# VectorE instead of adding DMAs for the low parts of chunk 1's second weight group and of chunk 6's GELU products

## The chip, the cores and the metric

The kernel runs on 1 core of one Trainium2 chip. The metric is the device time of one execution in microseconds (us), less is better. The kernel before took 605.02 us in the median of 3 runs (604.14 to 605.84).

The core has five engines that work side by side, each through its own list of instructions in order: TensorE (PE in the profile, its weight loads PEld), VectorE (DVE), ScalarE (ACT), GpSimd (POOL) and SyncE (SP). SP does nothing here but issue DMAs; POOL issues them too. An instruction waits for what it reads to be written and for the buffer that it writes to be free, and everything behind it on its engine waits with it.

## What is computed

The reference mixes two branches over the same input x (2048 tokens, 512 channels) with a gate for each token:

```python
x = A_x
g = _sigmoid((x * gate_w).sum(-1, keepdims=True))
a = _A_ref(x, A_wqkv, A_wo)                      # 32 heads of 16, 8 keys per query, 2 apart
b = _B_ref(x, B_w_gate, B_w_up, B_w_down)        # (gelu(x @ w_gate) * (x @ w_up)) @ w_down
return g * a + (1 - g) * b
```

`_A_ref` is an attention in which each query looks at 8 keys (itself and 7 earlier ones, every second token). `_B_ref` is a feed-forward layer with 1792 hidden channels. All is float32.

## The kernel before

**Two parities.** The tokens are split into even and odd ones (`par` 0 and 1), 1024 each, since the attention never crosses them. For each parity the kernel makes keys, queries and values, and then runs the feed-forward layer (`ffn(par)`), while VectorE works on attention in the background (scores L519 and L522, softmax L533 to L544, mixing L558 to L571). In the profile `ffn(0)` lies between about 50 and 283 us.

**High and low parts.** TensorE multiplies in a float32 format of reduced precision. So each operand is split into a high part (the number rounded to that format) and a low part (the rest), and a product is three matmuls: high by high, high by low, low by high. Where weights are split in `product`, the third matmul of each three is the first to use the weight's low part.

The low part is made in one of two ways:
- By VectorE: ACT copies the number to the high part, then VectorE subtracts that from the number.
- By an adding DMA: ACT copies the negated number to the place of the low part, POOL issues a DMA that adds the number to it, and ACT makes the high part with a second copy.

**Chunks.** `ffn` goes over 14 chunks (`f` = 0 to 13) of 128 hidden channels. A chunk is computed with a Strassen scheme in 7 products instead of 8; the weights of a chunk are therefore combined first (`combine`, three subtracts at L657 on VectorE) into seven pieces in two groups: `t1, t2, b11` (group 0) and `b21, t3, b22, t4` (group 1, 128x1024 elements). `operands(par, f, i)` splits group `i` of chunk `f` into tile `g0` or `g1`, in two steps. It is called one chunk ahead: the first step of group 1 is placed after the product `t1` and a piece of other work, the second after `s4`. In parity 0 group 0 is split by VectorE (L677, L681) and group 1 by an adding DMA (L685, L688, L690). Parity 1 reads group 0 back from DRAM, where parity 0 had stored it (`keep_parts`, L703), and its combined group 1 too (`keep`, L697).

**Buffers and queues around it.** The raw weights of a chunk lie in a tile `raw`, of which there are two. `fetch(f + 2)` (L647) loads the next but one into the same buffer, so it waits until chunk `f`'s last reader is done, the adding DMA and the store of `keep` included. SP issues that load, the loads `r` of the down weights (`fetch_d`, L651), the stores and the attention's loads in one queue. The adding DMAs are issued by POOL, whose transfers show as queue q0; SP's show as q1. POOL also issues adding writes of keys and queries to DRAM in chunks 0 and 1 (`key_one`, L465 and L466).

**GELU.** `gate_up` does the seven products of a chunk. L826 and L842 apply GELU to the gate's half, `add` (L740, L741) makes the up half. `hidden(par, (f, b), ge, up)` multiplies the two (L745) for each half `b` of the tokens and splits the product into `hh` and `hl`: for chunks in `LOWS[par]` by an adding DMA (L751 to L753), for others by VectorE (L748, L749). `down` (L776) multiplies them by the down weights `d`, a pair of chunks at a time; those are split in `down_w` by an adding DMA (L719, L720, L722), in the first chunks by VectorE (L715, L717).

**What sets the order.** The program text names no engine order by hand here: a scheduler orders the instructions on each engine. `paced` only keeps an instruction from being moved ahead of the last matmul emitted before it. A change of one instruction can therefore change the order of all that follow.

Of the kernel before, what the change touches and what calls it, by code (L numbers as in the profile page):

```python
# [33 lines left out]
LOAD = 4.0  # L34
BT = 4
MASKED = -1e9 * DH ** 0.5
LOWS = (4, 6, 8, 10), (4, 6, 8, 10, 12)


GROUPS = (("t1", "t2", "b11"), ("b21", "t3", "b22", "t4"))  # L40
# [5 lines left out]
def tile_gated_mix(ctx: ExitStack, tc: tile.TileContext, xt, wqkv, wff, wo, out):  # L46
# [11 lines left out]
    def tl(tag, dt=F32):  # L58
        return pool.tile([P, COLS.get(tag, 512)], dt, name=tag, bufs=BUFS[tag])
# [521 lines left out]
    def paced(ins):  # L581

        if PIN[0] and ins.ins.engine == mybir.EngineType.DVE:
            tc.keep_in_program_order(ins)
        if not PACING[0]:
            return ins
        tc.add_manual_dep(ins.ins, LAST[-1].ins.name, mybir.DependencyInfo(mybir.DependencyClass.Sync,
                          mybir.DependencyReason.SCHED_ONLY), reason="pace")
        return ins
# [72 lines left out]
    def operands(par, f, i):  # L662


        n = len(GROUPS[i]) * QW
        w = tl(f"g{i}", F32R)
        hi, lo = w[:, :n], w[:, n:2 * n]
        for k, op in enumerate(GROUPS[i]):
            WG[f, op] = hi[:, k * QW:(k + 1) * QW], lo[:, k * QW:(k + 1) * QW]
        if par and not i:  # L670
            nc.sync.dma_start(w[:, :2 * n].bitcast(F32), WS[f, i])
            yield
            return
        raw = RAW[f][:, 3 * i * QW:][:, :n]
        if not i:
            KEEP[f] = w[:, :2 * n]
            ins = nc.scalar.activation(hi, raw, AF.Copy)  # L677
            if f:
                paced(ins)
            yield  # L680
            ins = nc.vector.tensor_tensor(lo, raw, hi.bitcast(F32), op=OP.subtract)  # L681
            if f:
                paced(ins)
            return
        ins = nc.scalar.activation(lo, raw, AF.Copy, scale=-1.0)  # L685
        if par and not f:
            paced(ins)
        nc.gpsimd.dma_start(lo.bitcast(F32), raw, accum_op=OP.add)  # L688
        yield
        ins = nc.scalar.activation(hi, raw, AF.Copy)  # L690
        if par or f:
            paced(ins)
# [51 lines left out]
    def hidden(par, key, ge, up):  # L744
        nc.vector.tensor_tensor(ge, ge, up, op=OP.mult)  # L745
        hh_, hl_ = tl("hh", F32R)[:, :512], tl("hl", F32R)[:, :512]
        if key[0] not in LOWS[par]:
            nc.scalar.activation(hh_, ge, AF.Copy)  # L748
# [138 lines left out]
    def ffn(par):  # L887
        todo = iter(())
        for f in range(FC):
# [9 lines left out]
            if f + 1 < FC:  # L899
                for i in range(2):  # L900
                    steps = operands(par, f + 1, i)
                    at(1 + 2 * i, next, steps, None)
                    at(5 + i, next, steps, None)
                at(0 if f != 1 else 5, fetch_d, f + 1)
                for g_ in ((), (0, 1))[f] if f < 2 else (f,):
                    steps = down_w(par, g_)
                    at(2 if f > 2 else 4 - f % 2, next, steps, None)
                    at(7, next, steps, None)
            else:
                steps = down_w(par, f)  # L910
                at(1, next, steps, None)
                at(4, next, steps, None)
# [149 lines left out]
    for kc in range(KC):  # L1062
        name, i = ("b11", "b21")[kc // 2], kc % 2
# [134 lines left out]
    def first():  # L1198
        for _ in range(2):
            yield  # L1200
        combine(0)
        keep(0)
        for i in range(2):
            yield
            for _ in operands(0, 0, i):
                yield
        combine(1)
        fetch_d(0)
        yield
        for n in "t1", "b22":  # L1210
            room_b(n)
            for kc in range(2):
                if n == "t1":
                    combine_b("t1", "b11", "b22", "t2", kc)
                split_b(n, kc)
                yield
# [8 lines left out]
    def second():  # L1225

        yield from operands(1, 0, 0)
        room_v(*SMALL, *LARGE)
        for n in "b11", "b21", "t1", "b22", "t2":
            fetch_v(n)  # L1230
            yield
# [55 lines left out]
```

## Time and profile before

| | us |
|---|---|
| median of 3 runs | 605.02 |
| the profiled execution | 603.44 |
| its span, first to last instruction | 601.7 |
| TensorE busy | 589.1 |
| VectorE busy | 532.4 |
| ACT busy | 430.1 |
| POOL busy | 125.8 |

A row of the timeline has the start and the length in us, the engine, the line of the kernel and the operation, what it writes and reads, the shape and the count of equal instructions in a row; in square brackets stand the idle time before it and what ended that. Matmuls overlap: each is listed with its whole length, and the pace is read from start to start. The mean granted clock of TensorE over the span is 0.997 of full speed. The DMA rows have the queue, the packets, the MB moved and the time of the packets as a share of 16 DMA engines; shares of several queues can add to more than 100%, since packets of two queues overlap in an engine.

### The profile page before, as it was taken

What the parts mean: (1) busy time and instruction counts of PE and PEld (TensorE: products, weight loads), DVE (VectorE), ACT (ScalarE), POOL (GpSimd) and SP (SyncE); (2) the same over time, 40 slices, a digit from 0 to 9 for tenths busy, and PEclk for the clock granted to TensorE, in tenths of its full rate; (3) what the DMA queues carried; (4) which work ended last, traced back from release to release, by engine and by line L of the source; (5) the groups of instructions that cost most, each with busy time, mean ns of one, the idle gap of its engine ahead of it and who ended that gap; (6) DMA issues with size and microseconds to landing.
All of it is one profiled execution on the core that took longest, in us unless ns stands there. A gap on an engine that the chain in (4) does not pass through costs nothing.

```text
span 601.7 us, 8290 instructions
## 1 busy us (share of the span) xinstructions
PE 589.1 (98%) x2743; PEld 490.1 (81%) x2743; DVE 532.4 (88%) x619; ACT 430.1 (71%) x761; POOL 125.8 (21%) x147
## 2 busy tenths in 40 slices
PE   9999997999999999999999999999999999999997
PEld 7889885888878887888789888888888888887885
DVE  6979987999799998998896999799979988999891
ACT  6778783678796769767876665767696778796632
POOL 0131761112121202102100472112121212131200
PEclk9999999999999999999999999999999999999999
DMA  8689999988897979898889999689788988988724
GB/s 305 211 242 302 262 306 223 295 260 222 263 250 204 272 185 293 242 321 266 262 265 342 252 276 256 205 187 261 206 246 216 259 209 212 270 196 222 103 53 174
DMA packets 89896, 144.33 MB, mean 240 GB/s; under 512 B 8703, under 2 KB 50047, under 8 KB 89854
## 3 DMA queue, kind: packets, MB, share of 16 engines
q1 hardware_dynamic: 67470, 106.91, 54.5%
q0 software_dynamic: 22096, 36.51, 34.0%
q8 instruction: 21, 0.34, 0.2%
q10 hardware_dynamic: 288, 0.39, 0.2%
q14 instruction: 21, 0.17, 0.1%
HBM read 69.83 MB, written 46.49 MB: 193 GB/s over the span
## 4 chain that ended last, share of the span: by engine, by line
PE 78%; DMA 9%; issue 5%; ACT 5%; SPq 1%; DVE 1%; POOL 0%; POOLq 0%; ACTq 0%
PE p L729 35%; PE p L776 11%; PE acc L776 10%; PE acc L460 9%; PE p L1001 5%; DMA g<-raw 3%; PE acc L348 2%; PE p L348 2%; PE p L460 2%; PE acc L1001 2%; DMA r<-wff 1%; DMA raw<-ws 1%; DMA hl<-c 1%; DMA raw<-xt 1%; DMA raw<-wff 1%
## 5 line engine op out<-in xcount | busy, mean ns | idle before, releaser
L729 PE MATMUL p<-S,g 128*128 128x512 f32 x672 | 166.6, 389 | 0.2 <-ACT p L811 0.2
L729 PEld LDWEIGHTS p<-S,g 128*128 128x128 f32 x672 | 125.9, 188 | 26.6 <-ACT p L811 0.6
L729 PE MATMUL p<-A,g 128*128 128x512 f32 x504 | 127.4, 392 | 2.6 <-DMA g<-raw 2.6
L729 PEld LDWEIGHTS p<-A,g 128*128 128x128 f32 x504 | 95.4, 190 | 23.3 <-DMA g<-raw 3.4
L558 DVE TENSOR_TENSOR prod<-v,lg 128x2048 f32<-128x2048 f32 x32 | 72.9, 2279 | 0.9
L519 DVE TENSOR_TENSOR prod<-kq 128x2048 f32<-128x2048 f32 x32 | 73.0, 2280 | 0.3
L522 DVE TENSOR_REDUCE lg<-prod 128x128 f32<-128x2048 f32 x32 | 73.0, 2283 | 0.1
L776 PE MATMUL p<-d,hh 128*128 128x512 f32 x224 | 68.4, 390 | 1.9 <-ACT c L826 1.9
L688 POOL DMA_DIRECT2D g<-raw x28 | 24.2, 865 | 201.9 <-ACT g L685 142.3
L776 PE MATMUL acc<-d,hh 128*128 128x512 f32 x224 | 59.1, 391 | 0.0
L740 ACT ACTIVATE c<-p 128x512 f32<-128x512 f32 x56 | 33.5, 599 | 35.6 <-PE p L729 34.4
L776 PEld LDWEIGHTS p<-d,hh 128*128 128x128 f32 x224 | 42.0, 188 | 11.0 <-ACT c L826 2.4
L776 PEld LDWEIGHTS acc<-d,hh 128*128 128x128 f32 x224 | 42.0, 188 | 8.9 <-ACT hh L748 0.2
L741 DVE TENSOR_TENSOR c<-c,s 128x512 f32<-128x512 f32 x56 | 38.0, 686 | 10.4 <-ACT c L740 10.1
L745 DVE TENSOR_TENSOR c<-c 128x512 f32<-128x512 f32 x56 | 38.3, 686 | 5.2 <-ACT c L842 5.1
L776 PE MATMUL p<-d,hl 128*128 128x512 f32 x112 | 42.7, 390 | 0.0
L562 DVE TENSOR_TENSOR prod<-prod 128x1024 f32<-128x1024 f32 x32 | 39.1, 1221 | 0.3
L734 ACT ACTIVATE s<-p 128x512 f32<-128x512 f32 x56 | 33.0, 591 | 7.8 <-PE p L729 7.3
L720 POOL DMA_DIRECT2D d<-r x23 | 19.7, 857 | 88.5 <-ACT d L719 78.8
L789 ACT ACTIVATE rt<-p 128x512 f32<-128x512 f32 x48 | 28.3, 597 | 11.3 <-PE p L776 11.2
L460 PE MATMUL acc<-d,S 128*128 128x512 f32 x144 | 35.4, 390 | 0.6 <-ACT hh L1163 0.6
L776 PE MATMUL acc<-d,hl 128*128 128x512 f32 x112 | 34.9, 392 | 0.7 <-DMA hl<-c 0.7
(220 smaller groups left out, 1060.3 us busy)
## 6 DMA issues: line engine op xcount, KB each, us to landing
g<-raw POOLq DMA_DIRECT2D x28, 512.0 KB, 7.0
ws<-g SPq DMA_DIRECT2D x14, 768.0 KB, 7.5
g<-ws SPq DMA_DIRECT2D x14, 768.0 KB, 6.9
r<-wff SPq DMA_DIRECT2D x28, 256.0 KB, 4.6
raw<-wff SPq DMA_DIRECT2D x14, 512.0 KB, 4.4
d<-r POOLq DMA_DIRECT2D x23, 256.0 KB, 6.6
ws<-raw SPq DMA_DIRECT2D x14, 384.0 KB, 6.3
raw<-ws SPq DMA_DIRECT2D x14, 384.0 KB, 5.3
```

Of the source, the lines that this page charges most:

```text
L460: LAST[:] = [nc.tensor.matmul(ps, x[:, ts], w, start=(start and kc == i == 0), stop=(kc == 1 and i == 2), skip_group_check=True)]
L519: paced(nc.vector.tensor_tensor(prod, spans(k, jj), q[:, jj:jj + 2, None, :].to_broadcast([P, 2, W, UC]), op=OP.mult))
L522: nc.vector.tensor_reduce(two_of(lg, jj), prod.rearrange("p j w (h d) -> p (j w) h d", d=DH), axis=AX.X, op=OP.add)
L558: paced(nc.vector.tensor_tensor(prod.rearrange("p j w (h d) -> p (j w) h d", d=DH), spans(v, jj).rearrange("p j w (h d) -> p j w h d", d=D ...
L562: nc.vector.tensor_tensor(prod[:, :, :4], prod[:, :, :4], prod[:, :, 4:], op=OP.add)
L729: LAST[:] = [nc.tensor.matmul(ps, w_, a_, start=(start and kc == 0 and n == 0), stop=(kc == 1 and n == 2), skip_group_check=True)]
L734: nc.scalar.activation(s, ps, AF.Copy)
L740: nc.scalar.activation(c, ps, AF.Copy)
L741: nc.vector.tensor_tensor(c, c, s, op=OP.add)
L745: nc.vector.tensor_tensor(ge, ge, up, op=OP.mult)
L776: LAST[:] = [nc.tensor.matmul(pp, a[:, ts], w, start=(i == 0 and n == 0 and gr == 0), stop=(i == 1 and n == 2), skip_group_check=True)]
L1001: LAST[:] = [nc.tensor.matmul(pa, a, b, start=(first and n == 0), stop=(last and n == 2), skip_group_check=True)]
```

## The change

Group 1 of chunk 1 in parity 0 takes the same way as group 0: ACT copies to the high part in the first step, and VectorE subtracts in the second; the negated copy, the adding DMA and the later copy go. And chunk 6 leaves parity 0's list `LOWS`, so that both of its GELU products are split by VectorE. Parity 1 and all other chunks are as they were.

```diff
@@ -34,7 +34,7 @@
-LOWS = (4, 6, 8, 10), (4, 6, 8, 10, 12)
+LOWS = (4, 8, 10), (4, 6, 8, 10, 12)
@@ -674,6 +674,7 @@
         raw = RAW[f][:, 3 * i * QW:][:, :n]
         if not i:
             KEEP[f] = w[:, :2 * n]
+        if not i or (not par and f == 1):
             ins = nc.scalar.activation(hi, raw, AF.Copy)
             if f:
                 paced(ins)
```

From L677 on, a line of the kernel before has a number one higher in the kernel after.

## The prediction

> **What bounds the kernel now.** I read the page's busy times first, then TensorE's waits, then TensorE's timeline at the longest of them, then the clock by stretches.
>
> ```profile
> PE 589.1 (98%) x2743; PEld 490.1 (81%) x2743; DVE 532.4 (88%) x619; ACT 430.1 (71%) x761; POOL 125.8 (21%) x147
> ```
> ```profile
> PE p L729 <- DMA g<-raw: 2.6, 2, 1.5
> PE p L776 <- ACT c L826: 1.9, 1, 1.9
> PE acc L776 <- DMA hl<-c: 0.7, 1, 0.7
> ```
>
> TensorE is busy for all but 12.6 us of the span of 601.7, and the change touches no matmul. So the only gain is in TensorE's gaps, and the only loss is in new ones. The rows give total, times and longest; these three lie where the change acts or just behind it. The timeline of the worst place (start, length, engine, line, count):
>
> ```profile
> 92.25 0.61 PE L729 MATMUL p<-A,g 128*128 128x512 f32 x2
> 94.38 0.50 PE L729 MATMUL p<-A,g 128*128 128x512 f32 x1 [1.51 <-DMA g<-raw]
> ...
> 97.94 2.88 PE L729 MATMUL p<-S,g 128*128 128x512 f32 x12
> 100.66 0.39 PE L776 MATMUL acc<-d,hh 128*128 128x512 f32 x1
> 102.98 0.73 PE L776 MATMUL p<-d,hh 128*128 128x512 f32 x2 [1.93 <-ACT c L826]
> ...
> 105.36 4.05 PE L729 MATMUL p<-A,g 128*128 128x512 f32 x12
> 109.24 2.88 PE L729 MATMUL p<-S,g 128*128 128x512 f32 x12
> ```
> ```profile
> 100.00:104.00 4.00, 2.07 (x9) 1.40 (x8) 0.48 (x2) 2.19 (x5) 0.86 (x1) 1.00 0.50 197
> 104.00:108.00 4.00, 4.00 (x12) 3.16 (x11) 4.00 (x6) 2.34 (x4) 0.00 (x0) 0.57 0.88 206
> ```
>
> At full pace 12 matmuls start in 100.66 - 97.94 = 2.72 us, 0.227 each. The first gap is 94.38 - 92.25 less two matmuls: 1.68. The second is 102.98 - 100.66 less one: 2.09. Then comes a loss that no wait shows: from 104 to 108 the granted clock (third column from the end) is 0.57. From 102.98 to 109.24 run 20 matmuls, in 6.26 us for 4.53: 1.73 more. This place costs 1.68 + 2.09 + 1.73 = 5.5 us.
>
> The page "TensorE: Matmul & The Clock Gate" of the Trainium skill, section "Part 1: The HAM clock gate", says the clock halves after an idle window of about 3.4 us. Here a gap of 1.93 us, soon after one of 1.51, was followed by 0.57, so the trace does not need so long a gap. By the page's figure alone a shorter gap would cost no clock, and the place 3.8 us.
>
> **Why TensorE waits there.** The two gaps have one cause. POOL's, SP's and ACT's timelines:
>
> ```profile
> 58.88 0.86 POOL L688 DMA_DIRECT2D g<-raw  x1 [10.00 <-PE p L729]
> 80.22 0.89 POOL L688 DMA_DIRECT2D g<-raw  x1 [1.31 <-ACT g L685]
> ```
> ```profile
> 83.38 0.32 SPq L703 DMA_DIRECT2D ws<-g  x1
> 94.39 0.33 SPq L647 DMA_DIRECT2D raw<-wff  x1
> 94.77 1.34 SPq L651 DMA_DIRECT2D r<-wff  x2
> ```
> ```profile
> 101.81 0.63 ACT L719 ACTIVATE d<-r 128x512 fp32r<-128x512 f32 x1 [9.01 <-DMA r<-wff]
> 102.34 0.58 ACT L826 ACTIVATE c<-p 128x512 f32<-128x512 f32 x1
> ```
>
> The L688 issues at 58.88 and 80.22 are chunks 1 and 2. Chunk 2's adding DMA lands at about 94.3, and the third matmul of its "a12" product, the first to use a low part, starts at 94.38. SP's queue stands from 83.4 to 94.39 before L647, which needs the raw buffer that this DMA reads. Both r loads stand behind it, ACT's L719 waits 9.01 us for one, and the GELU L826 behind L719 frees TensorE's bank: the second gap.
>
> **The change, part 1: chunk 1.** Removed are one 128x1024 copy on ACT (L685) and one 0.52 MB adding DMA (58.88). The copy to the high part moves forward into L685's place; VectorE gets one 128x1024 subtract.
>
> ```profile
> L562 DVE TENSOR_TENSOR prod<-prod 128x1024 f32<-128x1024 f32 x32 | 39.1, 1221 | 0.3
> L749 DVE TENSOR_TENSOR hl<-c,hh 128x512 fp32r<-128x512 f32 x38 | 26.0, 686 | 1.9 <-ACT hh L748 1.9
> L685 ACT ACTIVATE g<-raw 128x1024 fp32r<-128x1024 f32 x28 | 29.5, 1054 | 4.4 <-DVE raw L657 2.3 <-DMA raw<-wff 2.0
> L751 ACT ACTIVATE hl<-c 128x512 fp32r<-128x512 f32 x18 | 11.3, 628 | 1.1 <-DVE c L745 1.1
> L752 POOL DMA_DIRECT2D hl<-c x18 | 16.8, 934 | 58.6 <-ACT hl L751 42.3 <-ACT hh L753 15.8 <-issue 0.6
> ```
>
> VectorE +1.22, ACT -1.05. In the changed program's order the subtract stands behind the second score reduction (63.29 below), so it ends near 66.7. TensorE's first use of it is in the product at 76.61: about 10 us of cover.
>
> ```profile
> 63.29 2.28 DVE L522 TENSOR_REDUCE lg<-prod 128x128 f32<-128x2048 f32 x1
> 78.70 0.95 DVE L681 TENSOR_TENSOR g<-raw,g 128x768 fp32r<-128x768 f32 x1
> ```
> ```profile
> 76.61 1.52 PE L729 MATMUL p<-A,g 128*128 128x512 f32 x6
> ...
> 84.09 1.07 PE L729 MATMUL p<-A,g 128*128 128x512 f32 x4
> ```
>
> What is queued behind it goes 1.2 us later. The nearest need is chunk 2's first low parts (L681, ending 79.65), used at 84.09: over 4 us of cover. Without that cover, each us late would be one on TensorE.
>
> What it frees is transfer time. The DMA rows (packets, MB, share of 16 engines) from 62 to 67 and 67 to 94, and chunk 2's issue (KB, us to landing):
>
> ```profile
> q0 software_dynamic: 144, 0.52, 52.5%
> ```
> ```profile
> q0 software_dynamic: 3830, 2.31, 62.5%
> q1 hardware_dynamic: 3262, 5.33, 57.2%
> ```
> ```profile
> g<-raw POOLq DMA_DIRECT2D x1, 512.0 KB, 14.1
> ```
>
> The 0.52 MB on q0 from 62 to 67 are chunk 1's DMA: 52.5% of 5 us = 2.6 us of all 16 engines. From 67 to 94 both queues together hold 120%: there is always work waiting, ending in chunk 2's 14.1 us. If all the freed time is passed on, chunk 2 lands 2.6 us earlier; if POOL's issue times set the pace, none. I take 1.8, nearer the full end, because the engines never run dry in between. ACT's copy for chunk 2 still stands just behind chunk 1's GELU L826, so its issue stays at about 80.
>
> The program's order on TensorE changes too: from chunk 1's last "S" products to that third matmul are 38 matmuls, not 43, so it is wanted 1.1 us sooner, at 92.70 - 1.13 = 91.6 (92.70 being 92.25 and two matmuls). From 94.4 to 91.6 are 2.8 us; less 1.8 leaves a gap of 1.0. One r load now stands before L647 on SP, and L826 before L719 on ACT. So the second gap has lost its cause, and with a gap of 1.0 I expect full clock: 4.5 of 5.5 us saved. Ends: all 2.6 passed on, 0.2 left, 5.3 saved; nothing passed on, a gap of 2.8 with 1.73 of clock, 1.0 saved.
>
> **Part 2: chunk 6.** Twice a 128x512 copy on ACT (0.63) and an adding DMA issued by POOL go; VectorE gets two subtracts of 0.69.
>
> ```profile
> 179.06 0.61 PE L729 MATMUL p<-A,g 128*128 128x512 f32 x2
> 180.32 1.19 PE L776 MATMUL acc<-d,hl 128*128 128x512 f32 x4 [0.65 <-DMA hl<-c]
> 181.35 0.62 PE L729 MATMUL p<-A,g 128*128 128x512 f32 x2
> ```
> ```profile
> 174.53 1.20 POOL L752 DMA_DIRECT2D hl<-c  x1
> ```
>
> Six matmuls take 2.29 us instead of 1.36: 0.9 lost to waiting for chunk 6's adding DMA. A subtract of 0.69 behind at most one attention step of 2.28 is sooner than the 5.8 us from that issue to that matmul. I take all 0.9; ends 0 and 0.9.
>
> **Part 3: the order.** No instruction is moved by hand, but from about 75 to 283 us nearly every engine's order differs. Besides the places above, that stretch loses this on TensorE:
>
> ```profile
> 233.04 0.61 PE L729 MATMUL p<-A,g 128*128 128x512 f32 x2
> 234.75 1.19 PE L729 MATMUL p<-A,g 128*128 128x512 f32 x4 [1.09 <-DMA g<-raw]
> ```
> ```profile
> 224.10 1.06 ACT L685 ACTIVATE g<-raw 128x1024 fp32r<-128x1024 f32 x1 [2.26 <-DVE raw L657]
> ```
>
> That is 1.71 less two matmuls, 1.3 us: VectorE combined chunk 11's weights late, so ACT and the adding DMA were late. A new order may keep this, lose it, or make another. I take 1.2 us of new loss, about one such event; ends: 1.3 gained, 6 lost (one more place like the first).
>
> **The sum.** 4.5 + 0.9 - 1.2 = 4.2 us. The profiled execution took 603.44 (span 601.7 and 1.74 around it), so 599.2 for its like. The median of the runs is 605.02, which gives 600.8.
>
> **Rivals.** (1) The transfer is not earlier: the first gap grows to 2.8 with slow clock and only the cascade behind it shrinks. For: the accumulating key and query writes ahead of chunk 2 on q0 are issued as TensorE yields them. Against: 120% from 67 to 94. Saved 1.0 + 0.9 - 1.2 = 0.7: 604.3, no change that can be told.
>
> (2) VectorE becomes the late engine. It is 88% busy and gets 2.6 us more. Place: chunk 11, where it already delays ACT by 2.26. If the combine is 2.6 later there, the gap grows from 1.3 to 3.9 and takes 1.73 of clock; a lag that reaches one more chunk costs a full 5.5. 4.5 + 0.9 - 2.6 - 1.73 - 5.5 = -4.4: 609.4. It decides once the third L657 of a chunk ends more than about 2 us behind ACT's readiness to copy. Against: VectorE has 69 us idle, and the 2.6 lie far before 224.
>
> Beside it, "SBUF — State Buffer" of the Trainium skill, section "Who interferes with whom", says that a VectorE instruction with two SBUF inputs contends with a GpSimd instruction that reads SBUF. The row of L752 above names no wait on VectorE, and I give it no price.
>
> **How the numbers follow.** Forecast 0.58, its own range 597.8 (5.3 + 0.9 and 1.0 of the old order's loss gone) to 603; rival 1 0.18; rival 2 0.20, in any size above 606.8 to 609.4 or lighter ones that only cancel the gain; 0.04 left. What a measurement can tell from no change is about 0.3%, 1.8 us. Faster takes the forecast and a fifth of rival 1: 0.62. Same takes most of rival 1 and the light cases of rival 2: 0.17. Slower: 0.21. The range 597.8 to 606.5 leaves out the heavy cases of rival 2 and little below.
>
> **What would show it.** Right: chunk 2's g<-raw lands by about 92.5, TensorE's wait for L826 is gone, no stretch near 104 has a clock under 1, and no wait for hl<-c near 180. Part 1 is wrong if that landing stays at 94. Part 3 is wrong if g<-raw or ACT waits over 2 us in all appear on TensorE between 110 and 283; if they follow L657, rival 2 holds.

## The result, and the profile after

| | before | after |
|---|---|---|
| median | 605.02 us | 597.30 us |
| lowest to highest of 5 runs | 601.82 to 606.29 | 596.79 to 598.35 |
| the profiled execution | 603.44 | 596.87 |
| its span | 601.7 | 595.1 |

The ratio is 0.9886, 95% interval 0.9861 to 0.991: faster, by 7.7 us between the medians and 6.6 us between the profiled executions. The forecast was 600.8 in a range of 597.8 to 606.5, so the direction was right; the median came out 0.5 us below the range, and by the ratio the time is 598.1, just inside it. Beside the experiments below, the kernel before had medians of 603.60 to 604.14 over 14 to 29 runs, so about 6.5 us is the safer figure for the gain.

The page of the kernel after, busy times:

```profile
PE 586.6 (99%) x2743; PEld 488.8 (82%) x2743; DVE 533.3 (90%) x622; ACT 429.4 (72%) x758; POOL 123.4 (21%) x144
```

VectorE is busy 0.9 us longer, TensorE 2.5 us shorter with the same 2743 matmuls: 1.7 of these are the low clock from 104 to 108 us before; where the rest lies isn't shown. Two of TensorE's waits (total, times, longest):

```profile
PE p L730 <- DMA g<-raw: 0.7, 1, 0.7
PE p L460 <- ACT p L434: 0.6, 1, 0.6
```

The waits for L826 and hl<-c are gone, and one of the two for g<-raw. TensorE's timeline at the place that was worst:

```profile
89.39 1.52 PE L730 MATMUL p<-S,g 128*128 128x512 f32 x6
90.74 0.61 PE L730 MATMUL p<-A,g 128*128 128x512 f32 x2
92.05 1.19 PE L730 MATMUL p<-A,g 128*128 128x512 f32 x4 [0.69 <-DMA g<-raw]
93.08 1.08 PE L777 MATMUL acc<-d,hh 128*128 128x512 f32 x4
```

The third "a12" matmul is wanted at 90.74 + 0.45 = 91.19 and starts at 92.05: a gap of 0.86 where there were 1.68 and 2.09. The stretches that answer to the two shown of before (column 3: TensorE's busy time; third from the end: granted clock):

```profile
100.00:104.00 4.00, 4.00 (x20) 3.30 (x19) 4.00 (x6) 1.70 (x3) 0.00 (x0) 1.00 0.72 174
104.00:108.00 4.00, 4.00 (x19) 3.34 (x18) 3.96 (x8) 3.33 (x6) 0.12 (x1) 1.00 0.97 349
```

Both are full, at full clock. The place now costs 0.86 us in place of 5.5. Further on, 110 to 283 us, in the kernel before and then in the kernel after:

```profile
110.00:283.00 173.00, 171.10 (x753) 140.71 (x752) 160.43 (x186) 132.37 (x221) 27.94 (x34) 1.00 0.91 255
```
```profile
110.00:283.00 173.00, 172.36 (x760) 142.18 (x759) 161.57 (x190) 134.40 (x223) 27.62 (x35) 1.00 0.90 254
```

The 0.64 us that the second lacks are the wait for L434 at the switch to parity 1, which the first has only after 283. So nothing is lost to chunks there any more, where before lost 1.9 (0.65 in chunk 6, 1.09 in chunk 11, the rest small).

**What moved.** POOL's, SP's and VectorE's timelines after:

```profile
81.10 0.89 POOL L689 DMA_DIRECT2D g<-raw  x1 [1.99 <-DMA v<-vs]
```
```profile
72.24 0.32 SPq L503 DMA_DIRECT2D v<-vs  x1
72.61 1.39 SPq L504 DMA_DIRECT2D v<-vs  x1
...
84.43 0.33 SPq L651 DMA_DIRECT2D r<-wff  x1
92.05 0.33 SPq L647 DMA_DIRECT2D raw<-wff  x1
92.48 0.41 SPq L651 DMA_DIRECT2D r<-wff  x1
```
```profile
65.85 1.22 DVE L682 TENSOR_TENSOR g<-raw,g 128x1024 fp32r<-128x1024 f32 x1
...
78.61 0.95 DVE L682 TENSOR_TENSOR g<-raw,g 128x768 fp32r<-128x768 f32 x1
```

Chunk 1's subtract ends at 67.07, and chunk 2's first low parts are no later than before (78.61 against 78.70). Chunk 2's adding DMA is issued 0.9 us later than before, yet lands 2.3 us earlier. The DMA rows from 62 to 67 us after show how:

```profile
q1 hardware_dynamic: 1656, 1.92, 105.4%
q0 software_dynamic: 8, 0.00, 1.0%
...
vs<-hh SPq DMA_DIRECT2D x5, 128.0 KB, 4.6
```

Before, chunk 1's DMA took 52.5% of the engines in this stretch, and SP's queue q1 these (same columns):

```profile
q1 hardware_dynamic: 695, 0.96, 53.2%
...
vs<-hh SPq DMA_DIRECT2D x2, 128.0 KB, 8.6
```

Without that DMA q1 moves twice the bytes, and the attention's stores vs<-hh land in 4.6 us instead of 8.6. The loads that follow those stores on SP (L503, L504) are issued at 72.24; before:

```profile
79.08 0.32 SPq L503 DMA_DIRECT2D v<-vs  x1
79.44 0.46 SPq L504 DMA_DIRECT2D v<-vs  x1
```

So 960 KB of loads that before were issued beside chunk 2's DMA (80.22) now go 7 us earlier, 9 us ahead of it.

The Trainium skill, "DMA: Bandwidth & Descriptors", section "Queues, rings and completion order", says that each DMA engine takes turns between the queues it has work for, packet by packet. The near equal halves of 52.5% and 53.2% while both queues had work agree with it.

### The profile page after: what moved, and what is told of

Same layout as the page of the kernel before. It is cut to its first block, busy times and chain, and to the rows that moved or that the text cites. A ratio compares the mean times of both kernels' runs of the same rounds, so it can differ in the third digit from the quotient of the medians.

```text
span 595.1 us, 8276 instructions
## 1 busy us (share of the span) xinstructions
PE 586.6 (99%) x2743; PEld 488.8 (82%) x2743; DVE 533.3 (90%) x622; ACT 429.4 (72%) x758; POOL 123.4 (21%) x144
## 4 chain that ended last, share of the span: by engine, by line
PE 90%; DMA 6%; DVE 1%; ACT 1%; issue 1%; SPq 0%; ACTq 0%; DVEq 0%
PE p L730 42%; PE p L777 13%; PE acc L777 12%; PE acc L460 10%; PE p L1002 5%; PE acc L348 3%; PE p L348 3%; DMA g<-raw 2%; PE acc L1002 2%; DMA v<-vs 1%; DMA raw<-ws 1%; PE p L460 1%; DMA vs<-hh 1%; DMA raw<-xt 1%; DVE raw L245 1%
## 5 line engine op out<-in xcount | busy, mean ns | idle before, releaser
L730 PE MATMUL p<-A,g 128*128 128x512 f32 x504 | 125.1, 390 | 0.7 <-DMA g<-raw 0.7
L730 PEld LDWEIGHTS p<-A,g 128*128 128x128 f32 x504 | 94.3, 188 | 20.8 <-DMA g<-raw 1.1
L460 PE MATMUL acc<-d,S 128*128 128x512 f32 x144 | 35.2, 390 | 0.6 <-ACT hh L1164 0.6
```

The lines of the kernel that those rows point to most:

```text
L460: LAST[:] = [nc.tensor.matmul(ps, x[:, ts], w, start=(start and kc == i == 0), stop=(kc == 1 and i == 2), skip_group_check=True)]
L730: LAST[:] = [nc.tensor.matmul(ps, w_, a_, start=(start and kc == 0 and n == 0), stop=(kc == 1 and n == 2), skip_group_check=True)]
```

## The experiments

All ratios are to the kernel before on the same chip; 0.001 is 0.6 us. The profile of a run is one execution.

### Each half alone

c1 changes only the condition in `operands`; c6 changes only `LOWS`.

```diff
+        if not i or (not par and f == 1):      (c1)
+LOWS = (4, 8, 10), (4, 6, 8, 10, 12)           (c6)
```

> Chunk 1's half of the change alone; chunk 6 keeps its adding DMAs. If chunk 1 carries the gain (theory): at the place near 92 us TensorE waits about 0.7 us for g<-raw, no wait for L827, no clock under 1, and 4.6 us or more are gained: ratio to before 0.989 to 0.993. A wait for hl<-c in chunk 6 may be there, up to 0.9 us. Rival, that chunk 6's half or the two together make the gain: ratio 0.996 or more.

> Chunk 6's half alone. Theory: the place of chunk 2 is as before, a gap of about 1.5 us for g<-raw, one of about 1.9 for L826 and a clock near 0.57 behind it; only up to 0.9 us near 180 and what the new order behind it does are gained: ratio 0.996 to 1.000. Rival, that chunk 6's half carries a good part: ratio 0.994 or less.

c1: 596.61 us median (596.46 to 599.95), ratio 0.9905 (0.9876 to 0.9935). c6: 602.73, ratio 0.9998 (0.9979 to 1.0017). Chunk 1's half carries the whole gain, and chunk 6's gives nothing that can be told. One thing of c1 was not as expected: its profile, at 599.95 the slowest of its 6 runs, has a gap of 1.85 us for g<-raw instead of about 0.7, with a clock of 0.89 and 0.68 in the two stretches from 92 to 100 us. The wait for L827 is gone in it. c6's waits on TensorE:

```profile
PE p L776 <- ACT c L826: 1.9, 1, 1.9
PE p L729 <- DMA g<-raw: 1.7, 1, 1.7
PE p L460 <- ACT p L434: 1.5, 1, 1.5
PE acc L348 <- ACT hl L355: 1.1, 1, 1.1
```

The two gaps near 92 us are as before, but this time full clock followed them, where 0.57 was expected. The wait for hl<-c is gone, and chunk 11's too, so with the clock some 4 us were won; but the order behind them changed, and the wait for L434 grew from 0.6 to 1.5, one of 1.1 for L355 is new, and after it 328 to 336 us ran at a clock of 0.84 and 0.73. The span came to 601.5 against 601.7.

### Is it the place of the r loads on SP?

rfirst is the kernel before with one dependency for the scheduler alone: chunk 4's raw load stays behind the r loads. Only SP's order differs from before.

```diff
+        if f == 4:
+            tc.add_manual_dep(ins.ins, RL[2].ins.name, ...SCHED_ONLY...)
```

> The kernel before with one thing changed: on SP's queue chunk 2's and chunk 3's r loads stand ahead of the raw load of chunk 4; nothing else is moved on any engine. Theory, that the second gap and the slow clock hang on the r load standing behind that raw load: the gap of 1.5 us for g<-raw stays, the one of 1.93 for L826 and the stretch with clock 0.57 go, 3.8 us gained: ratio 0.992 to 0.995. Rival, that the late adding DMA alone makes both gaps, or that r would land late anyway: ratio 0.998 to 1.000 and the wait for L826 still over 1 us.

Measured: 603.60 us, ratio 1.0012 (0.9989 to 1.0035). A miss: no gain. TensorE's waits and SP's timeline:

```profile
PE p L734 <- DMA g<-raw: 6.6, 2, 5.2
PE acc L781 <- DMA hl<-c: 1.2, 1, 1.2
```
```profile
82.83 0.32 SPq L503 DMA_DIRECT2D v<-vs  x1
...
84.80 0.92 SPq L656 DMA_DIRECT2D r<-wff  x2
98.47 0.33 SPq L647 DMA_DIRECT2D raw<-wff  x1
```

The wait for L826 is gone, as the prediction's step had it. But the 0.52 MB of r now travel beside chunk 2's DMA, which lands at about 98 instead of 94.3, and the first gap alone is 5.25 us. This profile is the slowest of its 12 runs (606.96), and the loads L503 too left 3.7 us later in it than before, so not all of that need be due to r; between the medians nothing is won or lost. Moving the r loads ahead is worth something only where the engines have room for them.

### Giving the transfer time back

The next five runs are the kernel after with something added in front of chunk 2's landing. None leaves out any of the computation.

```diff
             if f:
                 paced(ins)
+            if i:
+                extra = dram.tile([P, 4 * QW], F32, name="extra")
+                nc.gpsimd.dma_start(extra, raw, accum_op=OP.add)      (traffic, tclean)
+                nc.gpsimd.dma_start(extra[:, :2 * QW], raw[:, :2 * QW], accum_op=OP.add)      (half)
+                nc.sync.dma_start(extra, raw)      (bysp)
```

In traffic and bysp the scheduler also put chunk 3's r load ahead of chunk 4's raw load; tclean holds it behind, and rtwo has that move alone, with no added transfer.

> The kernel after, with a transfer of the size of chunk 1's removed adding DMA (0.52 MB, adding, issued by POOL in its old place, from the same buffer to a scratch area in DRAM that nobody reads). TensorE's, ACT's and VectorE's orders are those of after. Theory, that the freed transfer time lets chunk 2's adding DMA land sooner: it lands 1.5 us or more later than in after (near 94), TensorE's gap there grows from 0.7 us to 2 to 3, without a wait for L827; 1.5 to 3.5 us slower than after, ratio to before 0.991 to 0.995. Rival, that only the new order or POOL's issue times set the landing: it lands near 92, the gap stays 0.7, ratio 0.988 to 0.990.

> The kernel after with an unread adding transfer of half the size of the removed one (0.26 MB) in its place; every engine's order is that of after, SP's too. In the run with the full size a second r load also stood ahead of the raw load. Theory, shared transfer time: half the removed time comes back, chunk 2's adding DMA lands 1 to 2 us later than in after (92.05), TensorE's gap is 1.5 to 3 us, ratio to before 0.990 to 0.996. Rival, that the second r load made the loss in the full-size run: landing and gap as in after, ratio 0.987 to 0.990.

> The kernel after with the full-size unread transfer (0.52 MB), and chunk 3's r load kept behind the raw load and the next store on SP, so that one r load stands ahead as in after. Theory, shared transfer time: landing 2 us or more later than in after, gap 2.5 to 4 us with slow clock behind it, ratio to before 0.993 to 1.000. Rival, the second r load: ratio 0.987 to 0.990.

> The new kernel with an unread plain write of the same 0.52 MB (chunk 1's second group of raw, to a scratch in DRAM) issued by SP after chunk 1's sum store, in place of the unread adding transfer issued by POOL of the run named traffic. SP's order behind it is that of traffic (chunk 2's and chunk 3's r loads both ahead of chunk 4's raw load), and POOL's queue is that of the new kernel. It leaves nothing of the computation out. Theory (it is the transfer time of the 16 engines that the change gave back, whichever queue spends it, and the second r load ahead): chunk 2's adding DMA lands two to four us later than in the new kernel, ratio 0.996 to 1.001. Rival (it is the adding kind, or POOL's own queue, that makes the transfer dear): a plain write costs at most half as much, ratio 0.988 to 0.994.

> The new kernel with chunk 3's r load moved up beside chunk 2's, ahead of chunk 4's raw load on SP (one store moves ahead of that load with it); every other engine's order is that of the new kernel and no transfer is added. It separates the two things that the runs traffic and bysp changed at once. Theory (a transfer put onto the engines before chunk 2's adding DMA has landed delays it, whatever it is): 0.26 MB more ahead of the landing gives a gap of 1.5 to 3 us at the place near 92 us in place of 0.69, ratio 0.990 to 0.994. Rival (the r load costs nothing by itself, and the added transfers of traffic and bysp took the whole time): gap under 1 us, ratio 0.987 to 0.990.

| run | added ahead of the landing | L503 issued | chunk 2's DMA: issue, first use | gap by the wait | median | ratio (95%) |
|---|---|---|---|---|---|---|
| after | nothing | 72.24 | 81.10, 92.05 | 0.69 | 597.30 | 0.9886 (0.9861 to 0.991) |
| half | 0.26 MB adding | 72.95 | 83.36, 94.90 | 3.21 | 598.66 | 0.9912 (0.9888 to 0.9936) |
| rtwo | 0.26 MB, r load | 72.25 | 80.91, 93.43 | 1.93 | 599.31 | 0.9919 (0.9891 to 0.9947) |
| bysp | 0.52 MB plain, 0.26 MB r load | 74.81 | 81.64, 94.15 | 2.28 | 600.46 | 0.9951 (0.9935 to 0.9967) |
| tclean | 0.52 MB adding | 80.06 | 79.66, 95.36 | 3.93 | 601.83 | 0.9961 (0.9944 to 0.9978) |
| traffic | 0.52 MB adding, 0.26 MB r load | 80.75 | 80.33, 96.46 | 4.34 | 603.97 | 1.0014 (0.9994 to 1.0034) |

The profiles of half (slowest of 6 runs) and of tclean (slowest of 12) are slower than their medians, so their gaps are larger than the medians would make them; half's, 3.21, lies above what was expected. Traffic's row at the place, and bysp's:

```profile
96.46 2.07 PE L733 MATMUL p<-A,g 128*128 128x512 f32 x4 [4.34 <-DMA g<-raw]
```
```profile
94.15 2.05 PE L733 MATMUL p<-A,g 128*128 128x512 f32 x4 [2.28 <-DMA g<-raw]
```

What follows. An adding transfer that nobody reads and that no VectorE, ACT or TensorE instruction waits for gives about two thirds of the gain back by itself (tclean) and all of it with chunk 3's r load ahead (traffic), although VectorE still does the subtracts. So most of the gain is not in the engines' work but in the transfer. It isn't the raw buffer that the transfer holds either: in tclean it lands at 64.7 us, and the next raw load, at 72.33, waits for a store. The expectation of traffic was too small.

half does not show a dose, though it was meant to. POOL issued its transfer far ahead of the place of chunk 1's adding DMA (58.88), and it landed 8.4 us later, before the stores vs<-hh were issued. traffic's went 2.3 us ahead of the old place. The two issues, half's and traffic's:

```profile
48.28 1.22 POOL L683 DMA_DIRECT2D extra<-raw  x1
```
```profile
56.57 0.86 POOL L683 DMA_DIRECT2D extra<-raw  x1 [7.53 <-DMA vwt<-c]
```

In half L503 goes about when it goes in the kernel after (72.95 and 72.24), and the ratios of the two can't be told apart.

How the transfer is spent matters. Beside rtwo, which has their order of r loads, bysp's plain write costs 1.9 us and traffic's adding one 5.7; the first difference lies within the intervals, the second doesn't. bysp came out between the bands of its theory and its rival. By the rows of 62 to 67 us above, 0.52 MB takes 52.5% of 5 us = 2.6 us as an adding transfer, and as plain transfers 0.52/1.92 of 105.4% of 5 us = 1.4 us. The engines' time alone, 1.8 to 1, is less than the difference. bysp and traffic differ in kind, in queue and in the time of issue (63.60 against 56.57) at once, so which of these makes the adding one dear isn't shown.

The column of L503 is the likely rest. L503 waits for the last store vs<-hh: 5.9 us before, 2.9 after, 6.8 in tclean. Sorted by its issue, the six runs fall in two groups, and so do c1 (73.02), c6 (79.56), the kernel before (79.08) and rfirst (82.83): where the loads v<-vs go at 72 to 75, chunk 2's DMA needs 10.9 to 12.5 us from issue to first use; where they go at 79 to 83, 14.2 to 17.9.

The landings show the way between. Twelve adding writes of keys and queries (L465, L466) stand on q0 ahead of chunk 2's DMA, and in all ten profiles that DMA lands 2.3 to 3.3 us after the last of them (issue plus time to landing). The sixth lands no later before (80.8 us) than after (81.3), so by then nothing of chunk 1's DMA is felt on q0 itself; the twelfth lands at 91.7 before and 88.7 after. From the sixth to the twelfth q0 needs 7.4 to 9.1 us where L503 goes early, and 10.9 to 15.4 where it goes late, with the v<-vs loads beside it. The queues from 80 to 92 us, before and then after:

```profile
q0 software_dynamic: 1581, 1.05, 61.9%
q1 hardware_dynamic: 644, 2.51, 55.4%
```
```profile
q0 software_dynamic: 2245, 1.54, 90.0%
q1 hardware_dynamic: 444, 1.46, 33.1%
```

With 1.05 MB less on q1, q0 moves 0.49 MB more. The place of the loads was not changed by itself, so this link is read from ten profiles and not shown by an experiment of its own.

### Chunk 2's own group, and both

If chunk 2's DMA is what is late, VectorE can make chunk 2's parts instead. c2 does that in place of chunk 1; c12 does both chunks, c12b both without chunk 6's half, c13 chunks 1 and 3 without it.

```diff
+        if not i or (not par and f == 2):             (c2; LOWS as before)
+        if not i or (not par and f in (1, 2)):        (c12; LOWS as after)
+        if not i or (not par and f in (1, 2)):        (c12b; LOWS as before)
+        if not i or (not par and f in (1, 3)):        (c13; LOWS as before)
```

> The kernel before with chunk 2's second group, the one that TensorE waits for, made by VectorE instead of chunk 1's; chunk 6 as before. Theory, that chunk 2's late low parts are the whole place: no wait for g<-raw near 92, SP's raw load no longer stands behind that DMA, no wait for L826, ratio 0.988 to 0.993. Rival, that VectorE, full at that time, is late with the subtract or that the r loads are late anyway: ratio 0.996 or more.

> The kernel after with chunk 2's second group made by VectorE too. Theory: the last gap of 0.7 us for g<-raw is gone, ratio to before 0.985 to 0.989, at or below after. Rival, that VectorE's additional 1.2 us come late for TensorE, or the new order brings other waits: ratio 0.990 or more.

> Chunk 1's and chunk 2's second groups added by VectorE, chunk 6's low parts left with ACT as before. The run c12 lost its time at the switch to the second parity: no matmul of L460 lay between the last FFN matmuls and the first that needs ACT's L434, where the new kernel has 12 of 227 ns, and its wait there was 3.35 us against 0.64. Theory (that order alone makes c12 slower): here 8 matmuls lie there, so the wait is 0.64 + 4 x 0.227 = 1.5 us, no wait for g<-raw near 92, ratio 0.988 to 0.991. Rival (two groups on VectorE make it late elsewhere): waits for g<-c, hl or A parts between 70 and 280 us, ratio 0.993 or more.

> Chunk 1's and chunk 3's second groups added by VectorE, chunk 6's low parts left with ACT as before. In this order 24 matmuls of L460 lie ahead of the one that needs ACT's L434, so that the wait there (0.64 us in the new kernel, 3.35 in c12) should be nothing. Theory (the place near 92 us is mended by chunk 1's half, and what is left differs by the order at the switch): ratio 0.987 to 0.990. Rival (VectorE becomes the late engine with a second group): waits for DVE's parts, ratio 0.993 or more.

| run | median | ratio (95%) | span of the profile |
|---|---|---|---|
| c2 | 598.65 | 0.9923 (0.9892 to 0.9955) | 595.5 |
| c12 | 600.74 | 0.9939 (0.9916 to 0.9961) | 599.1 |
| c12b | 597.87 | 0.9910 (0.9890 to 0.9931) | 594.7 |
| c13 | 598.01 | 0.9918 (0.9892 to 0.9945) | 596.4 |

c2 mends the same place without touching chunk 1: in its profile TensorE has no wait for g<-raw at all, though L503 is issued at 78.70. That confirms what TensorE waited for. Its order has waits of its own further on, 1.9 us for L355 and 1.0 for L87. c12, with both, was expected to be the best and is the slowest of the four. Its timeline of TensorE at the switch to parity 1, and the granted clock there:

```profile
277.54 1.98 PE L460 MATMUL acc<-g,A 128*128 128x512 f32 x8
279.35 1.07 PE L777 MATMUL p<-d,hl 128*128 128x512 f32 x4
283.78 4.64 PE L460 MATMUL p<-d,A 128*128 128x512 f32 x10 [3.35 <-ACT p L434]
```
```profile
284.00:288.00 4.00, 4.00 (x10) 3.17 (x11) 4.00 (x8) 2.86 (x6) 0.07 (x1) 0.50 0.98 339
```

ACT evicts the last down products (L785) before it copies L434, which L460 waits for. In the kernel after, 12 matmuls of L460 lie between the last down product and that need; c12's order left none, so the wait is 3.35 us instead of 0.64, and the clock is 0.50 behind it. c12b's order leaves 8:

```profile
277.22 1.07 PE L777 MATMUL p<-d,hl 128*128 128x512 f32 x4
278.13 1.97 PE L460 MATMUL acc<-g,A 128*128 128x512 f32 x8
281.65 5.73 PE L460 MATMUL p<-d,A 128*128 128x512 f32 x24 [1.55 <-ACT p L434]
```

The wait is 1.55 where 1.5 was worked out ahead, and the ratio the upper end of what was expected. So the profiles show that c12 lost its time at a place 190 us further on, and not by two groups on VectorE. (c12b also leaves out chunk 6's half, and the intervals of the two overlap.) c13 has no wait there, but one of 1.1 for g<-raw and two of 0.6 and 0.4 in the last down products; its ratio lies just above its band. None of the four has a ratio below that of the kernel after. Only c12's interval lies wholly above the one of after; c2, c12b, c13 and c1, which has the lowest median of all (596.61), can't be told from it.

## Why the prediction was right, and where a size was off

- **What bounds the kernel** held: TensorE is at 99%, and all that was won was gaps and low clock.
- **Part 1** was right in size: 4.5 us forecast, 5.5 - 0.86 = 4.6 measured. Its terms: chunk 2's landing 1.8 us earlier, 2.3 measured; wanted at 91.6, 91.19 measured; a gap left of 1.0, 0.86 measured; clock 1.00 near 104, as forecast. Of its working one thing was simpler than the truth. It took the engines as one pool from which 0 to 2.6 us pass to chunk 2. The freed time went first to q1's stores and, through them, to loads that left before chunk 2's DMA was issued (at 81.10, not at about 80); and giving the 0.52 MB back cost 4.5 us (tclean against after), more than their own 2.6. So that 1.8 came near 2.3 is in part luck: the way to it was not the one that it was taken from. The full clock at the place wasn't sure either: c6 had it behind two gaps, and c1's profile lost it behind one of 1.85.
- **"So the second gap has lost its cause"** held after the change, but rfirst shows that the order alone is worth nothing. It needs the freed transfer time. ACT's timeline after, GELU first and no wait for r:

```profile
93.27 0.60 ACT L827 ACTIVATE c<-p 128x512 f32<-128x512 f32 x1
95.32 0.63 ACT L720 ACTIVATE d<-r 128x512 fp32r<-128x512 f32 x1 [1.45 <-PE acc L777]
```

- **Part 2**, 0.9 us: the wait for hl<-c went, in c6 too, but c6 as a whole gained nothing. It went in c1 as well, which keeps chunk 6's adding DMAs, and c1 is not slower than after. So the order that chunk 1's half makes was enough to remove it.
- **Part 3** is the term that was mis-sized: -1.2 forecast, about +1.3 measured. The new order lost nothing from 110 to 283, and chunk 11's gap of 1.3 went, which the prediction had as the good end of its bounds. ACT's copy for that chunk, in the timeline after, no longer waits for VectorE:

```profile
213.91 1.05 ACT L686 ACTIVATE g<-raw 128x1024 fp32r<-128x1024 f32 x1
```

 That gap is gone in c1 and in c6 as well, and is there in rfirst, whose other engines keep the old order (1.34 us). Both c1 and c6 give VectorE more work than before, so the gap was an accident of that order and not a cost of VectorE's load. With +1.3 in place of -1.2 the sum is 6.7, beside 6.6 measured between the profiled executions.
- The rest up to 7.7 us between the medians lies in the runs: the three behind the forecast had a median 1.6 above the profiled one, and the kernel after is 0.4 above its own.
- **Rival 1** (the transfer is not earlier) fell by the landing. traffic, at 603.97, comes near the 604.3 that it was put at, by a larger gap (4.34 us) than its 2.8. What it had in its favour, the key and query writes ahead of chunk 2 on q0, is the queue that the landing hangs on; but these writes too were through earlier. **Rival 2** (VectorE late) fell: chunk 11 has no wait, and c12b with chunk 2's group on VectorE too has none for g<-raw either. But c12 shows what the rival had right in kind: a new order can make a new place; c12's median is 3.4 us above that of the kernel after.

## What to carry to other kernels

Price a DMA that is taken away in a stretch where the queues are never empty by what it delayed, and not by its own bytes alone: find the next loads that were held up behind it, and the transfer that they then met. The cover of an instruction can stand; the order that the scheduler makes behind it can't be counted on, so look at each point where one engine's list must turn over to a new stage (here the switch to parity 1) and count the matmuls that lie between the last product and the first need. Two mends of one place don't add up: either chunk 1's or chunk 2's group was enough.

## What the runs showed of the hardware

The length of one gap doesn't decide the clock. In the kernel before gaps of 1.51 and 1.93 us within 11 us were followed by 0.57, in c6 gaps of 1.73 and 1.95 at the same place by full clock. In rtwo a gap of 1.93 us was followed by full clock; in c1 one of 1.85 was not (0.89 and 0.68 in the next two stretches), and in half one of 3.21 was followed by full clock up to 96 and then by this:

```profile
96.00:100.00 4.00, 4.00 (x12) 3.13 (x11) 3.83 (x3) 0.83 (x2) 0.00 (x0) 0.57 1.05 322
```

Bysp's row above shows four matmuls at half pace (2.05 us against 1.19) directly behind a gap of 2.28. The Trainium skill, "TensorE: Matmul & The Clock Gate", section "Part 1: The HAM clock gate", says that the window is free-running. A low clock now and then behind gaps of about 2 us, at once or later, agrees with that; its figure of one idle window of about 3.4 us does not, since gaps of 1.85 and 2.28 us were enough.

In the stretch from 62 to 67 us the adding transfer halved what SP's queue moved: 0.96 MB in 5 us against 1.92, at 53.2% and 105.4% of the engines. Stores of 128 KB in that stretch landed in 8.6 us instead of 4.6.
